# A new planned order, stores of two adjacent pieces in one transfer, and stores split over unequal row counts, in a cross-covariance attention with a mixture of adapters

## The chip, the cores and the metric

The kernel runs on one core of a Trainium2 chip. The metric is the device time of one execution in microseconds, lower is better. The core has five engines with their own instruction streams: TensorE (PE in the profile) for matrix products, VectorE (DVE), ScalarE (ACT), GpSimd (POOL) and SyncE (SP). The last two compute next to nothing here: GpSimd issues the loads and SyncE the stores. Sixteen transfer engines move the data between device memory and the on-chip memory.

## What is computed

Four batches of q, k and v, each of 6400 rows and 256 columns, are reduced to one 256 x 256 attention matrix per batch. Its product with v goes through a mixture of eight low-rank adapters, two of which are chosen for every row.

```python
qn = q / (np.linalg.norm(q, axis=1, keepdims=True) + 1e-06)     # norm over the 6400 rows
kn = k / (np.linalg.norm(k, axis=1, keepdims=True) + 1e-06)
s = kn.transpose(0, 2, 1) @ qn / tau                            # 256 x 256 per batch
a = softmax(s)                                                  # over the last axis
x = (v @ a).reshape(25600, 256)
logits = x @ w_gate                                             # 8 experts
topk, w = the two largest logits of a row, and their softmax
delta = sum over the two of w * (x @ A[e]) @ B[e]               # rank 16
out = x + delta
```

q, k and v are float32, 26.2 MB each, and so is the output of 26.2 MB. All of q and k of a batch must be there before its matrix a is known; only then can v of that batch be turned into output.

## The kernel before

**Tiling.** The 6400 rows of a batch are laid out as 128 partitions by 50 columns ("chunks"), each of 256 values; a column of all partitions is 128 KB in float32. q and k come in three loads each of 17, 17 and 16 columns (`QK`), some of them cut further (`PARTS`). v comes in five pieces of 10 columns (`NP`, `PC`). GpSimd's transfers convert to bf16 on the way (`do_load`). Output is written from y buffers of 10 columns in float32 (`do_store`), and goes out from SyncE, one store for each piece. The last two pieces of the last batch are stored in parts of 4, 4 and 2 columns (`FINE`, `UNITS`).

**Steps.** For q and k: `do_G` adds each chunk to the 256 x 256 product in two accumulators, and to the sums of squares, which are the diagonals of k'k and q'q. For the groups of chunks named in `OFF` these sums of squares are not made by TensorE but by ScalarE (`do_sq`), VectorE (`do_add`, `do_red`) and two small products (`do_n2p`). Then follow a short chain per batch (`n2`, `rsqrt`, `rq_ps`, `s`, `exp`, `aT_ps`, `waA_ps`, `waA`, `a`), which ends in the matrix a in bf16 and in its products with the gate's and the adapters' weights. For v: `T` transposes a piece, `ZL` (or `log` and `Z`) gives gate logits and adapter values, a few VectorE steps choose two experts, `Ze` weights the adapter values, `gzT` transposes them, `Y` makes the output of two chunks from four products of v with a and two with the adapters' B, and `Ye` copies it from PSUM into the y buffer. Pieces in `MERGED` make logits and adapter values in one product `ZL`; the others make `log` first and `Z` later. `Te`, `ZLe`, `gzTe` and `Ye` are copies that may go to ScalarE or VectorE, as the planner decides (`copy`).

**Order.** The order of every instruction is written out by a planner in the kernel file (class `Plan`), which runs when the program is built. It holds a cost for each step, a fixed number of buffers of each kind (`STORE`: 6 for q and k, 3 for v, 7 for y, and so on), and one rank for each step that follows from the order of the loads (`WORDS`) and from how far transposes run ahead (`AHEAD`). It then plays the kernel through; the order in which steps start in it is the order of the instructions, and the buffer that a step took in it is the buffer of the program. Transfers are modelled as two streams that share a rate. `WARM` matmuls on constant data are put in where TensorE would be idle, so that its clock stays up.

**Stores behind loads.** `HOLD` names stores that shall wait until a certain load has landed, so that this load and those ahead of it have the transfer engines for themselves. The kernel before does this with a transfer of its own: `do_hold` copies 16 values of the loaded tile into a scrap tile from SyncE, which must wait for the load, and stores stand behind it in SyncE's order:

```python
def do_hold(s, kind, b, i):
    ...
    nc.sync.dma_start(scrap, src)

def do_store(s, b, i, c, n):
    lo = i * PC + c
    nc.sync.dma_start(out_v[b, :, lo:lo + n, :], held["y", (b, i), ""][:, c:c + n, :])
```

**Queues.** Loads are issued in the order of `WORDS`; each waits on GpSimd until its buffer is free. Stores are issued in order on SyncE; each waits until its piece is complete. At most eight transfers of one issuing path are under way at once: a ninth waits until the one eight places ahead of it has landed.

Of the kernel before, what the change touches and what calls it, by code (L numbers as in the profile page):

```python
# [18 lines left out]
class Step:  # L19
# [3 lines left out]
    def __init__(self, key, eng, deps, rank, take, give, size=0.0):  # L23
        self.packet = max(size, 0.08)
        self.key, self.eng, self.deps, self.rank = key, eng, deps, rank
        self.take, self.give, self.size = take, give, size
        self.users, self.place = [], {}
        self.ready, self.end, self.on = 0.0, None, None
        self.left = len(deps)
        self.only = next(iter(eng)) if len(eng) == 1 else None  # L30


class Clock:


    WINDOW, FIRST, LOW, HIGH = 3.413, 0.31, 0.5, 0.8
# [32 lines left out]
class Plan:  # L69

    LAT = 0.07
    DMA_LAT = 1.8
    ENGINES = ("PE", "DVE", "ACT", "POOL", "SP")
    ISSUE = 0.55
    ISSUE_LAT = 1.8
    STORE_LAT = 1.4
    OUT = 8

# [15 lines left out]

    def run(self, head):
# [4 lines left out]
        loads, queue, stores = list(self.loads), [], []  # L100
        now, out, left = 0.0, 0, sum(s.key[0] != "warm" for s in self.steps.values())
        free["POOL"] = 0.2
        clock = Clock()

# [5 lines left out]
        def can_take(s):  # L110
            return all((kind, name) in held or self.store[kind] for kind, name in s.take)

        def start(s, eng):
            for kind, name in s.take:
                if (kind, name) not in held:
                    held[kind, name] = self.store[kind].pop(0)
                    s.place[kind] = held[kind, name]
            s.on = eng
            s.t = now
            self.out.append(s)  # L120

# [5 lines left out]
        while left:  # L127
            again = False
            if (loads and free["POOL"] <= now + 1e-9 and out < self.OUT and can_take(loads[0])):
                s = loads.pop(0)  # L130
                start(s, "POOL")
                out += 1
                free["POOL"] = now + self.ISSUE
                push(free["POOL"], "free", None)
                push(now + self.ISSUE_LAT, "asked", s)
                again = True
            for e in self.ENGINES:
# [3 lines left out]
                for s in wait[e]:  # L141
                    if not can_take(s) or (s.key[0] == "warm" and not clock.idle(now)):
                        continue
# [3 lines left out]
                    if best is None or (s.rank, s.seq) < (best.rank, best.seq):  # L147
                        best = s
# [9 lines left out]
                else:  # L158
                    push(free[e], "end", best)
# [3 lines left out]
            busy = [x for x in (queue, stores) if x]  # L163
            t = events[0][0] if events else float("inf")
            base = max(now, head)

            share = sum(x[0].packet for x in busy)
            if busy:
                t = min(t, base + min(x[0].size / x[0].packet for x in busy) * share)
            assert t < float("inf"), [s.key for s in self.steps.values() if s.end is None][:20]  # L170
            if t > base:
                for x in busy:
                    x[0].size -= (t - base) * x[0].packet / share
                    if x[0].size < 1e-6:
                        push(t + self.DMA_LAT, "landed", x[0])
                        out -= x is queue
                        x.pop(0)
            now = max(now, t)
            while events and events[0][0] <= now + 1e-9:
                _, _, what, s = heapq.heappop(events)  # L180
                if what == "asked":
                    queue.append(s)
                elif what == "store":
                    stores.append(s)
# [3 lines left out]
                elif what == "landed":  # L188
                    push(now + (SAFE if s.on == "POOL" else 0.0), "end", s)
                    for u in s.users:  # L190
                        if u.key[0] == "hold":
                            u.left -= 1
                            if u.left == 0:
                                push(now, "ready", u)
                elif what == "end":
# [6 lines left out]
                    for u in s.users:  # L202
                        u.left -= u.key[0] != "hold"
                        if u.left == 0 and u.eng and u.key[0] != "hold":
                            push(now + (0.0 if s.on == u.only else self.LAT), "ready", u)
# [10 lines left out]
V = ((0, 1), (1, 1), (2, 1), (3, 1), (4, 1))  # L216
# [13 lines left out]

def make_plan(B, order, ahead):
# [6 lines left out]
    for kind, b, i in order:  # L238
        if kind == "v":
            p.add(("load", "v", b, i, V[i][0] * PC, V[i][1] * PC), {}, (), 0, take=(("v", (b, i)),),  # L240
                  size=LOAD * V[i][1] * PC + 0.062)
            continue
        for c, n in PARTS.get((b, i), QK[i:i + 1]):
            for h in "qk":
                p.add(("load", h, b, i, c, n), {}, (), 0, take=(("qk", (h, b, i)),), size=LOAD * n + 0.062)

    for h in "qk":
        p.add(("cast", h), {"ACT": 0.6}, [("load", h, 0, 0) + PARTS[0, 0][0]], 0)
    p.loads[2].size += 0.5
    for b in range(B):  # L250

        for i, (c0, n) in enumerate(QK):
            for c in range(c0, c0 + n):
# [8 lines left out]
                p.add(("G", b, c), {"PE": 0.442 - 0.112 * sum((b, group_of(c), w) in OFF for w in "kq")}, deps,  # L262
# [4 lines left out]
        for w in "kq":  # L267
# [5 lines left out]
            for x, g in enumerate(halves):  # L273
                c, n = GROUPS[g]
                i = max(i for i, q in enumerate(QK) if q[0] <= c)
                p.add(("sq", w, b, g), {"ACT": 0.2 + 0.2125 * n},
                      [k for k in p.steps if k[:4] == ("load", w, b, i) and k[4] < c + n and c < k[4] + k[5]]
                      + [("cast", w)] * ((b, c) == (0, 0)), pos["qk", b, i] - SQ, take=(("ssq", (w, b)) if x == 0 else ("sq", (w, b, g)),),
                      give=(("qk", (w, b, i)),))
                if x:  # L280
                    p.add(("add", w, b, g), {"DVE": 0.15 + 0.268 * n},
# [4 lines left out]
            if halves:  # L286
                p.add(("red", w, b), {"DVE": 1.9}, [before], pos["qk", b, len(QK) - 1] - 1, give=(("ssq", (w, b)),))
# [699 lines left out]
```

## Time and profile before

| | |
|---|---|
| time, median of three runs | 254.41 us (254.39 to 254.47) |
| span of the profiled run | 252.7 us |
| TensorE busy (matmul) | 217.8 us, 86% |
| VectorE busy | 192.7 us, 76% |
| ScalarE busy | 151.1 us, 60% |
| loads: share of the 16 transfer engines | 74.4%, 6,912 packets |
| stores and small transfers: share | 26.1%, 3,968 packets |
| device memory read and written | 78.91 MB and 26.21 MB, 416 GB/s over the span |

The span is the time from the first to the last instruction of the profiled execution. The share of a queue is the time that its packets took, as a share of sixteen engines over the span; packets of one engine may overlap a little, so the sum can pass 100%. A packet of a load or a store is one row: what one partition receives or gives in one transfer. The bytes of a load are counted as written, in bf16, while twice as many are read. A line such as "POOL v L578 <- PE T_ps L788" means that an instruction of GpSimd which writes v, from line 578, stood idle until an instruction of TensorE that writes T_ps was done.

### The profile page before, as it was taken

To read this page: it belongs to the slowest core of one execution; us is meant where nothing else is said; L and a number is where in the kernel's file an instruction comes from. 1 tells how busy PE (TensorE), PEld (TensorE's weight loads), DVE (VectorE), ACT (ScalarE), POOL (GpSimd) and SP (SyncE) were. 2 spreads that over 40 slices of the span, in tenths; PEclk is the share of its full clock that TensorE was granted. 3 is DMA by queue.
4 is the path that set the end of the run, shared out by engine and by line. 5 is a ranking of instruction groups with operands and counts; after the bars stand their busy time and mean duration, and the time that the engine had idled before them with its cause. 6 is when DMAs were issued, how large, how long until landed. Compare 5 with 4: busy or idle time off the path is not lost.

```text
span 252.7 us, 5852 instructions
## 1 busy us (share of the span) xinstructions
PE 217.8 (86%) x2357; PEld 193.0 (76%) x2357; DVE 192.7 (76%) x528; ACT 151.1 (60%) x269; POOL 27.1 (11%) x54
## 2 busy tenths in 40 slices
PE   0274995988999998689999999889999979999990
PEld 0162882876999996579899899779999769999980
DVE  0055589869899987588899899489898898889850
ACT  5454427546786543975667768362674846657671
POOL 7003010040002002000500100500000000000000
PEclk9998899999999999999999999999999999999997
DMA  8999999999999999999999999999999999999996
GB/s 251 217 217 209 211 223 208 217 218 215 215 217 241 303 305 298 224 213 221 210 215 220 215 217 217 211 212 313 317 251 353 322 341 317 337 392 415 404 408 249
DMA packets 11243, 66.70 MB, mean 264 GB/s; under 512 B 1360, under 2 KB 1744, under 8 KB 6608
## 3 DMA queue, kind: packets, MB, share of 16 engines
q0 software_dynamic: 6912, 38.80, 74.4%
q1 hardware_dynamic: 3968, 26.87, 26.1%
q10 hardware_dynamic: 336, 0.66, 0.8%
q8 instruction: 18, 0.29, 0.4%
q14 instruction: 9, 0.07, 0.1%
HBM read 78.91 MB, written 26.21 MB: 416 GB/s over the span
## 4 chain that ended last, share of the span: by engine, by line
PE 53%; DMA 32%; issue 5%; DVE 4%; ACT 2%; POOL 1%; POOLq 0%; DVEq 0%
DMA v<-in_v_dram 18%; PE Y_ps L915 13%; PE acc L593 10%; DMA qk<-in_q_dram 10%; PE Y_ps L920 6%; PE T_ps L788 5%; PE ZL_ps L812 5%; DMA qk<-in_k_dram 5%; PE gzT_ps L902 4%; PE acc L597 3%; PE acc L602 2%; PE Z_ps L879 1%; ACT a_exp L715 1%; DVE a_bf L763 1%; PE log_ps L826 1%
## 5 line engine op out<-in xcount | busy, mean ns | idle before, releaser
L593 PE MATMUL acc<-qk 128*128 128x256 bf16 x400 | 69.6, 282 | 17.0 <-DMA qk<-in_k_dram 9.4
L915 PE MATMUL Y_ps<-a_bf,vT 128*128 128x256 bf16 x400 | 60.0, 273 | 0.2 <-DVE acc_sb L710 0.2
L621 DVE TENSOR_TENSOR ssq<-ssq,sq 128x1280 f32<-128x1280 f32 (+1 forms) x27 | 43.4, 1606 | 19.6 <-ACT sq L615 19.6
L769 ACT COPY y<-Y_ps 128x512 f32<-128x512 f32 x79 | 46.2, 586 | 16.6 <-PE Y_ps L920 13.5
L593 PEld LDWEIGHTS <-qk 128*128 128x128 bf16 x400 | 34.2, 101 | 20.7 <-DMA qk<-in_k_dram 11.5
L615 ACT ACTIVATE sq<-qk 128x1280 f32<-128x1280 bf16 (+1 forms) x27 | 36.9, 1368 | 17.7 <-DVE ssq L621 16.6
L915 PEld LDWEIGHTS <-vT 128*128 128x128 bf16 x400 | 38.9, 98 | 4.7 <-issue 0.3
L920 PE MATMUL Y_ps<-ball,gzT 128*128 128x256 bf16 x200 | 38.2, 273 | 0.0
L597 PE MATMUL acc<-qk 128*128 128x128 bf16 x242 | 34.5, 224 | 0.0
L788 PE MATMUL T_ps<-ident,v 128*128 128x128 f32 x200 | 27.6, 274 | 0.6 <-DVE waA_sb L757 0.4
L769 ACT COPY vT<-T_ps 128x512 f32<-128x512 f32 (+1 forms) x44 | 21.2, 510 | 10.9 <-PE T_ps L788 10.5
L597 PEld LDWEIGHTS <-qk 128*128 128x128 bf16 x242 | 24.4, 101 | 3.5
L890 DVE TENSOR_TENSOR gz<-zl,gateg 128x256 bf16<-128x256 f32 x70 | 26.3, 445 | 0.3
L578 POOL DMA_DIRECT2D v<-in_v_dram x20 | 11.5, 576 | 133.7 <-PE T_ps L788 92.8
L788 PEld LDWEIGHTS T_ps<-ident,v 128*128 128x128 f32 x200 | 22.3, 141 | 1.6 <-DVE waA_sb L757 0.6
L602 PE MATMUL acc<-qk 128*128 128x128 bf16 x168 | 23.4, 222 | 0.0
L902 PE MATMUL gzT_ps<-ident,gz 128*128 128x128 f32 x100 | 20.9, 281 | 2.6 <-DVE gateg L868 1.4
L920 PEld LDWEIGHTS <-gzT 128*128 128x128 bf16 x200 | 19.6, 98 | 2.3
L812 PE MATMUL ZL_ps<-waA_sb,vT 128*128 128x136 bf16 x280 | 19.5, 223 | 1.7 <-DVE waA_sb L757 1.5
L771 DVE COPY gzT<-gzT_ps 128x256 f32<-128x256 f32 (+1 forms) x40 | 15.0, 380 | 7.1 <-PE gzT_ps L902 5.6
L812 PEld LDWEIGHTS <-vT 128*128 128x128 bf16 x280 | 17.7, 98 | 2.4 <-issue 2.1
L615 ACT ACTIVATE ssq<-qk 128x1536 f32<-128x1536 bf16 x8 | 11.9, 1489 | 11.4 <-DMA qk<-in_q_dram 7.4
(80 smaller groups left out, 271.3 us busy)
## 6 DMA issues: line engine op xcount, KB each, us to landing
out_dram<-y SPq DMA_DIRECT2D x18, 1280.0 KB, 16.7
v<-in_v_dram POOLq DMA_DIRECT2D x20, 640.0 KB, 20.5
qk<-in_q_dram POOLq DMA_DIRECT2D x7, 1088.0 KB, 23.7
qk<-in_k_dram POOLq DMA_DIRECT2D x7, 1088.0 KB, 28.4
qk<-in_q_dram POOLq DMA_DIRECT2D x4, 512.0 KB, 19.2
qk<-in_k_dram POOLq DMA_DIRECT2D x4, 512.0 KB, 22.5
qk<-in_q_dram POOLq DMA_DIRECT2D x2, 1024.0 KB, 19.4
qk<-in_k_dram POOLq DMA_DIRECT2D x2, 1024.0 KB, 23.8
```

The source lines that it names most:

```text
L593: nc.tensor.matmul(acc[ic][:, 0:256], kt[:, j, ic::CC], qt[:, j, :], start=c == 0, stop=False, skip_group_check=True)
L597: nc.tensor.matmul(acc[ic][:, 256:384], kt[:, j, ic::CC], kt[:, j, ic::CC], start=False, stop=False, skip_group_check=True)
L602: nc.tensor.matmul(acc[ic][:, 384:512], qt[:, j, ic * P:(ic + 1) * P], qt[:, j, ic * P:(ic + 1) * P], start=False, stop=c == NC - 1, skip_ ...
L615: nc.scalar.activation(out[:, 0:n, :], t[:, j:j + n, :], ACT.Square)
L621: nc.vector.tensor_tensor(out=t, in0=t, in1=held["sq", (w, b, g), ""][:, 0:n, :], op=OP.add)
L769: nc.scalar.copy(out, in_)
L788: nc.tensor.matmul(ps[:, j, :], vt[:, c + j, :].bitcast(FP32), W["ident32"], is_transpose=True, start=(j == 0), stop=(j == n - 1))
L812: nc.tensor.matmul(ps[:, j, :], vT_of(b, i, c + j)[:, :, ic], st[b]["waA"][:, ic, :], start=(j == 0 and ic == 0), stop=(j == n - 1 and ic ...
L890: nc.vector.tensor_tensor(out=pairs[:, h].rearrange("p c (e r) -> p c e r", e=E), in0=z[:, 2 * h:2 * h + 2, :].rearrange("p c (e r) -> p c ...
L902: nc.tensor.matmul(ps[:, j, :], pairs[:, j * P:(j + 1) * P], W["ident32"], is_transpose=True, start=(j == 0), stop=(j == n // 2 - 1))
L915: nc.tensor.matmul(ps[:, j, :], vT_of(b, i, c + j)[:, :, ic], st[b]["a"][:, ic, :], start=(j == 0 and ic == 0), stop=False, skip_group_che ...
L920: nc.tensor.matmul(ps[:, j, :], pair[:, :, j], W["B"], start=False, stop=(j == 1), skip_group_check=True)
```

## The change

The transfers and the planner that orders everything are changed; the arithmetic is the same.

- Five pairs of adjacent pieces (`PAIRS`) take two adjacent y buffers and leave in one store of 20 columns. For that, all y buffers become one tile and all v buffers another, and the planner looks for adjacent free places (`find`).
- Three entries in `SPLIT` name stores that leave in four transfers of 112, 6, 6 and 4 rows (`SHARES`), to give transfer engines unequal shares.
- `HOLD` is new in content, and a held store now depends on the load itself, without a transfer of its own.
- The planner's model of transfers follows single rows of two rings in turn, with a cost for each row and for each completion, and a spread of completions that grows with time. Its costs of steps are revised.
- The order of loads (`WORDS`), the sets `OFF` and `MERGED`, and the constants `AHEAD`, `SQ`, `SAFE` and `HEAD` are new.

The diff, cut to its core:

```diff
+PAIRS = {(0, 3), (1, 1), (1, 3), (2, 0), (3, 1)}
...
+def pieces(b, i):
+    return next((((b, j), (b, j + 1)) for j in (i - 1, i) if (b, j) in PAIRS), ((b, i),))
...
-            parts = UNITS if b == B - 1 and i >= NP - FINE else ((0, PC),)
+            names = pieces(b, i)
+            if (b, i) != names[0]:
+                continue
+            parts = UNITS if b == B - 1 and i >= NP - FINE else ((0, PC * len(names)),)
...
-WORDS = ('q10 v00 v01 v02 q11 v03 q12 v04 v10 v11 q20 v12 v13 v14 q21 v20 v21 v22 q22 q30 '
-         'q31 q32 v23 v24 v30 v31 v32 v33 v34')
+WORDS = ('q10 v00 v01 q11 v02 v03 q12 v04 q20 v10 q21 v11 q22 v12 v13 v14 v20 q30 q31 v21 v22 q32 v23 v24 v30 '
+         'v31 v32 v33 v34')
-AHEAD = 2.7
+AHEAD = 1.9
-HOLD = {(0, 0): ('k', 3, 1), (0, 1): ('k', 1, 2), (0, 4): ('k', 3, 2), (1, 0): ('k', 3, 1),
-        (1, 1): ('k', 3, 2), (1, 2): ('k', 3, 2), (1, 3): ('k', 3, 2), (1, 4): ('k', 3, 2),
-        (2, 0): ('k', 3, 1), (2, 1): ('k', 3, 2), (2, 4): ('k', 3, 1)}
+HOLD = {(0, 0): ('v', 3, 4), (0, 1): ('k', 3, 0), (0, 2): ('k', 3, 0), (0, 3): ('v', 3, 2), (0, 4): ('v', 1,
+        4), (1, 0): ('v', 1, 3), (1, 1): ('v', 1, 3), (1, 2): ('k', 1, 0), (1, 3): ('v', 2, 3), (1, 4):
+        ('v', 3, 1), (2, 0): ('v', 2, 4), (2, 2): ('v', 1, 3), (3, 2): ('v', 3, 2), (3, 3): ('v', 3, 4), (3,
+        4): ('v', 2, 3)}
+SPLIT, SHARES = {(0, 0), (1, 4), (3, 0)}, (112, 6, 6, 4)
...
-SQ = 2
-SAFE = 0.5
+SQ = 4.0
+SAFE = 2
...
+    Y = sbuf.tile([P, STORE["y"] * PC, C], FP32, name="y")
+    VS = sbuf.tile([P, STORE["v"] * PC, C], BF16, name="v")
...
-        nc.sync.dma_start(out_v[b, :, lo:lo + n, :], held["y", (b, i), ""][:, c:c + n, :])
+        at_y = at["y", (b, i)] * PC + c
+        p = 0
+        for rows in SHARES if (b, i) in SPLIT else (P,):
+            r = nc.sync.dma_start(out_v[b, p:p + rows, lo:lo + n, :], Y[p:p + rows, at_y:at_y + n, :])
+            if (b, i) in HOLD and not p:
+                tc.add_manual_dep(r.ins, loaded[held_by(plan, b, i)],
...
+            p += rows
```

`OFF` goes from 35 entries (195 chunk sums) to 33 (185), `MERGED` from 14 pieces to 13. The first loads are the same in both: four columns of q and of k from SyncE and ScalarE, the other thirteen from GpSimd.

In the order that the planner makes, the stores of the kernel before begin with the pieces (0,2), (0,1), (0,3), (0,0), (1,0) and (2,0), batch first, and go on in order from (0,4). Those of the changed kernel are: (1,0); (1,1) with (1,2); (0,1); (0,2); (1,3) with (1,4); (2,0) with (2,1); (2,2); (2,3); (0,3) with (0,4); (2,4); (3,0); (0,0); (3,1) with (3,2); and then (3,3) and (3,4) in parts of 4, 4 and 2 columns.

## The prediction

> **What bounds the kernel now.** I read the page's slices and queues first, then the windows at the head, in the middle and at the tail, then the chain and the waits. The page shows what the transfer engines do over the whole span:
>
> ```profile
> PE   0274995988999998689999999889999979999990
> DMA  8999999999999999999999999999999999999996
> GB/s 251 217 217 209 211 223 208 217 218 215 215 217 241 303 305 298 224 213 221 210 215 220 215 217 217 211 212 313 317 251 353 322 341 317 337 392 415 404 408 249
> q0 software_dynamic: 6912, 38.80, 74.4%
> q1 hardware_dynamic: 3968, 26.87, 26.1%
> HBM read 78.91 MB, written 26.21 MB: 416 GB/s over the span
> ```
>
> The DMA row is full from the second slice to the last but one, and the loads' share and the stores' share add up to 100.5% of 16 engines' span. A pure load stretch shows some 215 GB/s because a load is counted at its two-byte size; it reads twice that. TensorE is also near full from about 100 us on, but a single engine at 86% beside a queue at 100% says that transfers come first. The windows show where the transfer engines are not full (columns: stretch, length, busy time of the engines, clock, DMA share, GB/s):
>
> ```profile
> 0.00:1.00 1.00, 0.00 (x0) 0.00 (x0) 0.00 (x0) 0.00 (x0) 0.20 (x4) 1.00 0.05 4
> 1.00:2.00 1.00, 0.00 (x0) 0.00 (x0) 0.00 (x0) 0.19 (x1) 0.58 (x1) 1.00 0.80 127
> ...
> 110.00:160.00 50.00, 49.61 (x533) 45.52 (x531) 42.87 (x106) 34.50 (x62) 4.77 (x9) 1.00 1.04 216
> ...
> 238.00:239.00 1.00, 1.00 (x18) 0.99 (x16) 0.71 (x2) 0.77 (x3) 0.00 (x0) 1.00 0.83 338
> 239.00:240.00 1.00, 1.00 (x13) 0.90 (x11) 1.00 (x4) 0.17 (x1) 0.00 (x0) 1.00 0.85 356
> ...
> 249.00:250.00 1.00, 0.00 (x0) 0.00 (x0) 0.00 (x0) 0.00 (x0) 0.00 (x0) 0.59 0.85 338
> 250.00:251.00 1.00, 0.00 (x0) 0.00 (x0) 0.00 (x0) 0.00 (x0) 0.00 (x0) 0.50 0.34 133
> 251.00:252.00 1.00, 0.00 (x0) 0.00 (x0) 0.00 (x0) 0.00 (x0) 0.00 (x0) 0.50 0.06 25
> ```
>
> Three gaps are to be seen. The head costs 0.95 + 0.20 = 1.15 us. Near 239 us there is a hole of about 0.17 + 0.15, with the 0.90 share of the next window some 0.4 us in all. At the tail the 16 engines don't end together: from 249.0 on the mean engine works 0.85 + 0.34 + 0.06 = 1.25 us, so it ends at 250.25, and the slowest at about 251.5. The semaphore records agree: the last store's 16 completions come between 249.95 and 251.95 us, ten of them 0.37 to 2.00 us after the first, six within 0.15 us. So in a kernel that is bound by transfers the end is set by the mean work of an engine, by holes, and by how far the slowest engine lags.
>
> The chain and one wait:
>
> ```profile
> 246.55 0.23 PE Y_ps L920 x2
> 246.78 0.02 issue
> 246.81 0.59 ACT y L769
> ```
>
> ```profile
> POOL v L578 <- PE T_ps L788: 92.8, 11, 17.7
> ```
>
> TensorE ends at 246.78, the last copy into y at 247.40 and the span at 252.7: both resources end together, transfers a little later. GpSimd's long waits for T cost nothing as long as the DMA row stays full, which it does.
>
> **What the Trainium skill says.** "DMA: Bandwidth & Descriptors", section "Issuing engines are not separate DMA queues", says that transfers of all issuers run on the same 16 engines and interleave. The trace agrees: the two queues' shares add up to one full set. The same page, section "Specifications", puts HBM at about 358 GB/s for one core and the fabric at 435; the trace has 416 over the span and 2 x 216 = 432 in loads, so the second is the nearer ceiling and I take measured rates. Section "Why a DMA increments its semaphore by 16 and not by 1" says that a transfer issued by SyncE uses the largest count of engines up to 16 that divides its rows, the lowest-numbered ones. No transfer of the kernel before shows that split at this size: 112 rows would be 7 on each engine, 6 rows one each on engines 0 to 5, 4 rows one each on 0 to 3. Section "Queues, rings and completion order" says that an engine takes turns between its rings by packet; a 20-column row would then hold up a load row for longer.
>
> **The change, part by part.**
>
> Pairs. Five pairs become one store each, so each engine moves 40 rows fewer, of twice the size. What a row costs beyond its bytes is taken from the trace's packet records: over 5 us windows a store row of 10,240 bytes takes 390 ns of an engine's time, while load rows read 26.9 bytes per ns, which would be 381 ns; store rows of 4,096 and 2,048 bytes (about 167 and 84 ns) are 15 and 8 ns over the same line. So 9 to 12 ns a row, and 40 rows give 0.36 to 0.48 us. I take 0.45. No 20,480-byte row is in the trace; the lower bound is 0.
>
> Split stores. SPLIT names (0,0), (1,4) and (3,0), but (1,4) is the second piece of the pair (1,3), and its store carries the name (1,3): in the program built from the change only two stores of 112 rows stand on SyncE. Each takes a row (0.39 us) from engines 6 to 15 and gives two to engines 0 to 3 and one to 4 and 5. Over two stores: -0.78, +1.56 and +0.78 us. If the six early engines of the trace are 0 to 5, the late ten end at up to 2.00 - 0.78 = 1.22 us and the early four at about 1.56, so the last completion comes 2.0 - 1.6 = 0.4 us earlier. If a late engine is among 0 to 3, it ends at up to 3.5, which is 1.5 later. That engine numbers can't be seen in this trace is the largest unknown; six being early, as the shares suppose, speaks for the first. I take -0.4.
>
> Order. Loads carry the same bytes; the seven v loads behind the last q and k are the same. The hole at 239 us is a store that was not ready; with stores kept back for the end (the store of (0,0) waits for the last v load) I expect most of it filled: -0.3 us, bounds 0 and -0.4.
>
> Holds. Three transfers of 32 bytes and the SyncE waits for them go; the waits now sit on the stores themselves. Stores queue in order on SyncE, so what stands behind a held store waits too, and through y slots so does the copy of Y. Six small extra transfers of 0.33 us issue each are hidden behind stores of 3 us. Together 0.
>
> TensorE and the others. OFF drops from 195 to 185 chunk sums, each worth two 128-column matmuls (0.11 us): +1.1 us. MERGED drops from 14 to 13; a merged piece has twenty ZL matmuls in 1.18 us, another one log 0.50 and Z 1.12: +0.4. Warm-up matmuls fall from 39 to 19. TensorE is idle or warming up for some 43 us of the span, so 1.5 us can be hidden; behind the last waA_ps the work falls from 40.1 to 38.8 us, because five instead of three of the last seven pieces are merged. Twenty gzT copies move from VectorE (76% busy) to ScalarE (60%). I put these at 0 for the end.
>
> The sum: -0.45 - 0.4 - 0.3 = -1.15. I give 0.1 back for the pair of (3,1) and (3,2), which can't start until both pieces are done. The span is 1.7 us shorter than the time in both (252.7 against 254.41), so the forecast is 254.4 - 1.05, about 253.4 us.
>
> **Rivals.**
>
> TensorE becomes the end. After Y of (3,2) it has 9.9 us of work (ten Y groups of 0.655, T, ZL and gzT), while transfers still to come are 40 columns, 12.5 us at 3.12 per ten. With 0.6 us to the copy's end and 1.2 from issue to first packets (the head's 1.15), the mean engine can't end before TensorE's end + 0.6 + 1.2 + 12.5 - 9.9, that is 4.4 us behind it; today it ends 3.5 behind. A gain of 0.75 in the mean asks TensorE to end at about 245.1 instead of 246.8. For it: the shorter tail, and loads of batch 3 that come earlier in the new order. Against: more work in all, and full windows from 110 us on. If it ends where it does now, the mean engine ends 0.9 later and the skew gives 0.4 back; halfway between is about 254.3, no change.
>
> A hole in the middle. Stores now begin behind the load of (1,3), near 122 us by the load order at 3.06 us per ten columns, where they began at 76.6. Until then y's seven slots fill; once they are full, Y stops, vT and v slots stay taken, loads stop, and held stores may not fill the gap. Against it: the kernel before kept the queue full through 92.8 us of such waits. One hole of 2 to 3 us, or a split that falls on the late engines, gives about 255.7, slower.
>
> All of it is had: 0.48 + 0.4 + 0.4, and a skew that falls by 0.3 more, gives 252.8.
>
> **How the numbers follow.** The forecast of about 253.4 has 0.5, the full gain 0.13, TensorE at the end 0.17, a hole or a wrong split 0.2. Under 253.9 lie the first two and a little of the third: faster 0.66. The rest of the third within half a microsecond of now, with a little of the fourth: same 0.14. Slower 0.2. The range leaves out half of the slow case and the very best: 252.6 to 255.4.
>
> **What would show it.** Right: store packets of 20,480 bytes near 765 to 775 ns; a DMA row without a hole at 239 us; the last store's completions within 1.6 us; TensorE ending near 245.3. Wrong: a DMA share under 0.9 between 80 and 240 us; GpSimd waiting for T or SyncE for a held load while that share is low; completions spread by 3 us; TensorE ending at or after 246.8.

## The result, and the profile after

The changed kernel takes 258.16 us (median of 4 runs, 257.86 to 258.56) where the kernel before takes 254.4: a ratio of 1.0148, with a 95% interval of 1.0131 to 1.0166. It is 3.8 us slower. The forecast was 253.4, and the time lies outside the range of 252.6 to 255.4 too.

The page of the changed kernel, with the rows that answer to those shown of before:

```profile
PE   0774995899999899889999995899899899999960
...
DMA  8999999999999999999999999999999999999696
GB/s 248 210 217 207 214 220 213 222 217 208 218 214 216 213 217 217 217 213 212 214 309 215 216 329 322 317 288 214 215 298 391 342 315 316 422 302 352 271 389 242
...
q0 software_dynamic: 6912, 38.80, 73.6%
q1 hardware_dynamic: 3184, 26.87, 25.9%
...
HBM read 78.91 MB, written 26.21 MB: 409 GB/s over the span
```

The span is 256.8 us. The load packets (second column of a queue) are as many as before, the store packets 784 fewer, and the bytes the same. The work of the transfer engines did fall. This is an estimate from the packet records: if every packet is charged the time that its kind takes undisturbed, an engine's mean work is about 248.4 us before and 247.9 after. But the DMA row now has a 6 in the third slice from the end, and TensorE's clock is at half near 160 us. The windows show both (columns: stretch, length, busy time of PE, PEld, DVE, ACT and POOL, clock, DMA share, GB/s):

```profile
160.00:168.00 8.00, 6.55 (x53) 5.92 (x54) 2.96 (x3) 4.22 (x7) 0.00 (x0) 0.57 1.03 316
232.00:234.00 2.00, 2.00 (x30) 1.94 (x28) 1.27 (x5) 1.93 (x6) 0.00 (x0) 1.00 1.02 404
234.00:236.00 2.00, 2.00 (x21) 1.78 (x20) 1.76 (x9) 1.54 (x4) 0.00 (x0) 1.00 1.06 336
236.00:238.00 2.00, 2.00 (x21) 1.91 (x19) 1.97 (x6) 1.51 (x4) 0.00 (x0) 1.00 0.71 256
238.00:240.00 2.00, 2.00 (x30) 1.97 (x28) 1.52 (x5) 1.91 (x6) 0.00 (x0) 1.00 0.34 132
240.00:242.00 2.00, 2.00 (x21) 1.79 (x20) 1.76 (x10) 1.54 (x5) 0.00 (x0) 1.00 0.61 236
254.00:256.00 2.00, 0.00 (x0) 0.00 (x0) 0.00 (x0) 0.00 (x0) 0.00 (x0) 0.50 0.15 59
```

From 232 us on only stores are under way. At full rate they move about 430 GB/s: 433 in the window from 234 to 236 us of e1_unsplit below, and sixteen rows of 10,240 bytes in 385 ns are 426. So 336, 256, 132 and 236 mean that (94 + 174 + 298 + 194) / 430 x 2 us = 3.5 us are lost between 234 and 242. TensorE is busy in all of it: the data are being made. For the most part a transfer is missing, and SyncE's own instructions say why. This is the line of the stores, from 232.5 us to the issue of the pair (3,1) and (3,2) (count, then shortest, median and longest duration in ns):

```profile
L973 SPq DMA_DIRECT2D out_dram<-y x5: 322/1552/2811, 232.5 to 239.2; - x5
```

One by one, from the records of SyncE (start and duration in us):

```
store          rows   start   took        store          rows   start   took
(3,0)          112   225.24   0.34        (0,0)          112   232.55   0.32
(3,0)            6   225.64   1.66        (0,0)            6   232.91   2.81
(3,0)            6   227.35   1.38        (0,0)            6   235.77   1.81
(3,0)            4   228.77   1.39        (0,0)            4   237.63   1.43
                                          (3,1)+(3,2)    128   239.17   1.55
```

The parts of six and four rows keep SyncE for 1.4 to 2.8 us each. The pair is complete at 237.8 us, but SyncE is free for it only at 239.1, its issue takes 1.55, and its first rows start at 241.2. Then forty columns of stores follow, 12.5 us at 3.12 per ten, and the first completion of the last store comes at 254.24. TensorE ends at 248.06 and the last store is issued at 248.7, so the end is set by what is queued, not by TensorE.

A missing transfer is not all of it. In the window from 234 to 236 us the DMA share is 1.06 and yet only 336 GB/s are moved: the engines are busy there, with rows that take too long. The packet records tell the two parts of the loss apart. Behind the last row of a load, where only stores are under way, a row of 10,240 bytes takes 385 ns in the median, before and after. Before, 4 of 798 such rows took over 450 ns; in the changed kernel it is 27 of 243, the longest 1.96 us. What they took beyond 385 ns is 0.96 us for the mean of sixteen engines (0.06 before), and from 231.9 to 242 us the mean engine has no packet under way for 2.65 us (0.36 before). Together this is the loss of 3.5 us.

This is the end of the chain of waits, and GpSimd's wait for T, against 246.78 and 92.8 us before:

```profile
247.84 0.23 PE Y_ps L962 x2
248.09 0.59 ACT y L812
```

```profile
POOL v L629 <- PE T_ps L830: 111.0, 13, 26.1
```

GpSimd's waits for T are 18 us longer. Between 130 and 212 us they cost as little as before: with packets charged as above, no stretch of 2 us there is used by less than 0.98. The stretch ahead of it, from 124 to 128 us, comes up again below.

### The profile page after: what moved, and what is told of

Same layout as the page of the kernel before. It is cut to its first block, busy times and chain, and to the rows that moved or that the text cites. A ratio compares the mean times of both kernels' runs of the same rounds, so it can differ in the third digit from the quotient of the medians.

```text
span 256.8 us, 5860 instructions
## 1 busy us (share of the span) xinstructions
PE 221.6 (86%) x2377; PEld 196.3 (76%) x2377; DVE 177.4 (69%) x501; ACT 157.0 (61%) x289; POOL 27.2 (11%) x54
## 4 chain that ended last, share of the span: by engine, by line
DMA 43%; PE 29%; issue 13%; DVE 8%; ACT 2%; POOL 2%; POOLq 0%; ACTq 0%
DMA qk<-in_k_dram 28%; DMA v<-in_v_dram 15%; PE Y_ps L957 8%; PE Y_ps L962 4%; PE ZL_ps L854 4%; PE acc L644 3%; PE T_ps L830 3%; PE gzT_ps L944 3%; DVE ssq L672 3%; POOL qk L629 1%; PE acc L653 1%; DVE ssq L678 1%; DVE gz L932 1%; PE Z_ps L921 1%; PE acc L648 1%
## 5 line engine op out<-in xcount | busy, mean ns | idle before, releaser
L644 PE MATMUL acc<-qk 128*128 128x256 bf16 x400 | 75.5, 286 | 17.4 <-DMA qk<-in_k_dram 10.9
L672 DVE TENSOR_TENSOR ssq<-ssq,sq 128x1280 f32<-128x1280 f32 (+1 forms) x25 | 40.4, 1615 | 29.3 <-ACT sq L666 27.7
L644 PEld LDWEIGHTS <-qk 128*128 128x128 bf16 x400 | 35.7, 104 | 21.2 <-DMA qk<-in_k_dram 12.6
L666 ACT ACTIVATE sq<-qk 128x1280 f32<-128x1280 bf16 (+1 forms) x25 | 34.4, 1374 | 23.5 <-DVE ssq L672 10.9
L957 PEld LDWEIGHTS <-vT 128*128 128x128 bf16 x400 | 39.3, 99 | 4.2
L653 PE MATMUL acc<-qk 128*128 128x128 bf16 x252 | 36.2, 227 | 0.0
L812 ACT COPY vT<-T_ps 128x512 f32<-128x512 f32 (+1 forms) x47 | 23.9, 533 | 14.1 <-PE T_ps L830 13.6
L830 PE MATMUL T_ps<-ident,v 128*128 128x128 f32 x200 | 29.5, 274 | 0.8 <-DMA v<-in_v_dram 0.8
L648 PE MATMUL acc<-qk 128*128 128x128 bf16 x178 | 27.1, 237 | 0.0
L653 PEld LDWEIGHTS <-qk 128*128 128x128 bf16 x252 | 23.8, 102 | 1.9
L932 DVE TENSOR_TENSOR gz<-zl,gateg 128x256 bf16<-128x256 f32 x65 | 23.5, 445 | 0.4
L812 ACT COPY gzT<-gzT_ps 128x256 f32<-128x256 f32 (+1 forms) x40 | 13.4, 346 | 14.4 <-PE gzT_ps L944 14.1
L648 PEld LDWEIGHTS <-qk 128*128 128x128 bf16 x178 | 19.3, 108 | 3.8
```

The source lines that it names most:

```text
L644: nc.tensor.matmul(acc[ic][:, 0:256], kt[:, j, ic::CC], qt[:, j, :], start=c == 0, stop=False, skip_group_check=True)
L648: nc.tensor.matmul(acc[ic][:, 256:384], kt[:, j, ic::CC], kt[:, j, ic::CC], start=False, stop=False, skip_group_check=True)
L653: nc.tensor.matmul(acc[ic][:, 384:512], qt[:, j, ic * P:(ic + 1) * P], qt[:, j, ic * P:(ic + 1) * P], start=False, stop=c == NC - 1, skip_ ...
L666: nc.scalar.activation(out[:, 0:n, :], t[:, j:j + n, :], ACT.Square)
L672: nc.vector.tensor_tensor(out=t, in0=t, in1=held["sq", (w, b, g), ""][:, 0:n, :], op=OP.add)
L812: nc.scalar.copy(out, in_)
```

## The experiments

The theories of the loss are these. A: the small parts of split stores hold SyncE, and what stands behind them comes late; the rivals within it are that they are slow because they use fewer than sixteen engines, or because one transfer follows close on another. B: TensorE comes late and sets the end. C: the rows of 20,480 bytes hold up loads that TensorE waits for. D: TensorE's half clock near 160 us (the first window above, clock 0.57) makes everything late. E: these loads are late because stores share the engines with them at all. F and G: the hold on store (1,0) and the pair at the end leave holes of their own. Ratios below are to the kernel before, with 95% intervals. Where the intervals of two runs overlap, their difference is not clear of noise. This holds of e2_unpair, e3_warm and e13_smallfirst against the changed kernel, and of e6_split16, e7_tail and e9_split22 against e1_unsplit.

**Whole stores (e1_unsplit).** Program order of all engines stays.

```diff
-SPLIT, SHARES = {(0, 0), (1, 4), (3, 0)}, (112, 6, 6, 4)
+SPLIT, SHARES = set(), (112, 6, 6, 4)
```

> The changed kernel, order kept, with the two stores of 112, 6, 6 and 4 rows sent whole again. Theory A: the small transfers of 6 and 4 rows occupy SyncE for 1.4 to 2.8 us each, six in a row before the pair of (3,1) and (3,2), and hold that pair back to 239.2 us although its last copy ended at 237.8. Then all issues take about 0.35 us, the pair is issued near 237.9, its packets begin near 239, the hole from 236 to 242 us shrinks by 1.5 to 2.5 us, and the time falls from 258.2 to about 256.0. Theory B: the end is set by TensorE, which comes about 3 us late out of a load of k that lands at 161.4 us; the small transfers only fill time. Then TensorE still ends at 248.1 and the time stays at 257.6 or more.

Measured: 255.39 us (254.65 to 257.5, 17 runs), ratio 1.0046 (1.0029 to 1.0064). So the six extra transfers cost 2.8 us of the 3.8. TensorE ends at 247.46, only 0.6 us earlier, so B falls. The stores' line, and five windows:

```profile
L973 SPq DMA_DIRECT2D out_dram<-y x19: 332/333/913, 124.2 to 248.1; - x19
```

```profile
124.00:126.00 2.00, 2.00 (x29) 1.92 (x27) 2.00 (x3) 1.24 (x4) 0.83 (x2) 1.00 1.04 185
126.00:128.00 2.00, 2.00 (x32) 1.95 (x30) 1.93 (x8) 1.76 (x2) 1.02 (x2) 1.00 1.10 179
...
234.00:236.00 2.00, 2.00 (x21) 1.80 (x19) 1.82 (x8) 1.48 (x4) 0.00 (x0) 1.00 1.05 433
236.00:238.00 2.00, 2.00 (x21) 1.96 (x20) 1.97 (x7) 1.93 (x4) 0.00 (x0) 1.00 0.70 296
238.00:240.00 2.00, 2.00 (x30) 1.91 (x28) 1.45 (x6) 1.60 (x5) 0.00 (x0) 1.00 1.16 492
```

The median issue is 0.333 us now, the pair goes out at 237.2, and the slow rows are gone (1 of 265 over 450 ns): from 234 to 236 us the share is as in the changed kernel, and the rate 433 GB/s instead of 336. Two holes stay: near 237 us, and at 124 to 128, where loads alone move 185 and 179 GB/s instead of 216. The DMA share is above 1 in the latter all the same: packets that share an engine overlap in the record, so a hole in a stretch of loads shows in the GB/s column.

**Split stores in the kernel before (e5_before_split).** Its stores (2,4) and (3,0) leave in 112, 6, 6 and 4 rows.

```diff
-        nc.sync.dma_start(out_v[b, :, lo:lo + n, :], held["y", (b, i), ""][:, c:c + n, :])
+        p = 0
+        for rows in (112, 6, 6, 4) if (b, i) in ((2, 4), (3, 0)) else (P,):
+            nc.sync.dma_start(out_v[b, p:p + rows, lo:lo + n, :], held["y", (b, i), ""][p:p + rows, c:c + n, :])
+            p += rows
```

> The kernel before, with the stores of (2,4) and (3,0) alone sent in 112, 6, 6 and 4 rows. There the next store on SyncE comes some 6 us later each time, so that up to 5 us of issue should be hidden. Theory A: each transfer of 6 or 4 rows takes 1.2 to 2.8 us of SyncE here too, against 0.33 for the others. On shares there are two readings: if the early engines are the low-numbered ones, as the change supposes, the 16 completions of the last store close up from 2.0 to about 1.6 us and the time is 254.0 to 254.2; if not, they spread to 2.5 us or more and the time is 254.9 or more; the same time as before would mean that the shares don't reach the end.

Measured: 256.46 us (256.39 to 257.0), ratio 1.0081 (1.0068 to 1.0094): 2.1 us slower than without the split. But the issues are short, and a wait stands in their place:

```profile
L930 SPq DMA_DIRECT2D out_dram<-y x9: 252/322/426, 219.3 to 236.4; - x9
```

```profile
SPq L930 <- DMA out_dram<-y: 8.6, 3, 3.2
```

```profile
234.00:236.00 2.00, 2.00 (x27) 1.88 (x26) 1.86 (x6) 1.28 (x3) 0.00 (x0) 1.00 0.93 323
236.00:238.00 2.00, 2.00 (x21) 1.82 (x19) 1.48 (x7) 1.80 (x4) 0.00 (x0) 1.00 0.90 317
```

A small part takes one of the eight places like a large one. At 230.4, 233.5 and 236.4 us SyncE waited for the transfer eight places ahead to land (8.6 us in all), so the store of (3,1), issued at 233.2 us in the kernel before, went at 236.4. Yet these waits cost next to nothing in the sum: from 231.9 to 242 us the mean engine has nothing under way for 0.40 us, where it was 0.36, since the hole that the kernel before had near 239 is gone. Two other things cost. 54 of 794 rows behind the last load are slow, 1.02 us for the mean engine against 0.06; that is why the windows show 323 and 317 GB/s at shares of 0.93 and 0.90. And the last store's completions are spread over 3.4 us, the last of them 2.2 us behind their mean, where it was 1.3. The two come to 1.9 us. Whether the shares fall on engines that lag already isn't shown, since the records don't number the engines. So splitting lost here in two ways, neither of them slow issue.

**Parts of 112 and 16 rows (e6_split16).** Sixteen rows use all sixteen engines; the part leaves sixteen completion records.

```diff
-(112, 6, 6, 4)
+(112, 16)
```

> The changed kernel, order kept, with the two split stores in 112 and 16 rows instead of 112, 6, 6 and 4: both parts can use all 16 engines, a row on each. Theory A1: it is the transfer with fewer than 16 engines that is slow to issue; then every issue takes 0.33 to 0.5 us, the pair of (3,1) and (3,2) is issued near 238, and the time is that of the unsplit order, 255.2 to 255.8. Theory A2: any further transfer behind a full queue is slow to issue; then the 16-row parts take 1.2 us or more each, and the time is 256 to 257.

Measured: 256.34 us (255.55 to 256.67), ratio 1.0062 (1.0045 to 1.0079), between whole stores and four parts. The two parts of 16 rows took 0.62 and 2.16 us to issue. So it isn't the number of engines below sixteen that makes a part slow. Nor is SyncE what costs here: it is free at 233.9, and the pair goes out at 236.1, earlier than in e1_unsplit. The engines are busy and move too little, where they move some 430 GB/s with whole rows:

```profile
234.00:236.00 2.00, 2.00 (x21) 1.88 (x19) 1.89 (x6) 1.48 (x5) 0.00 (x0) 1.00 1.01 358
236.00:238.00 2.00, 2.00 (x30) 1.99 (x29) 1.52 (x6) 1.91 (x6) 0.00 (x0) 1.00 0.98 363
```

Rows are slow again, 30 of 261 behind the last load, and the last store's completions are spread over 3.5 us instead of 1.8.

**Small parts first (e13_smallfirst).**

```diff
-(112, 6, 6, 4)
+(4, 6, 6, 112)
```

> The changed kernel with the parts of its two split stores the other way round, 4, 6, 6 and then 112 rows. If a small part is slow to issue because a large part was issued just before it, the first small ones now take 0.25 to 0.45 us, SyncE is free for the pair (3,1) and (3,2) at about 237.8 and the time is 255.4 to 256.5. If any transfer of less than 16 engines that comes close behind another is slow there, three of the four of each store still take 1.4 to 2.8 us: 257.5 to 258.6, as in the changed kernel.

Measured: 257.72 us (257.13 to 260.01), ratio 1.0142 (1.0106 to 1.0179), as slow as the changed kernel. The issues of (3,0) took 0.33, 0.61, 0.63 and 0.57 us, those of (0,0) 0.25, 1.55, 1.26 and 0.62. The first of a store is quick and those close behind it are not, the large part among them. The pair is out at 236.7, earlier than in e1_unsplit, and yet there is a hole, earlier too:

```profile
234.00:236.00 2.00, 2.00 (x21) 1.81 (x19) 1.86 (x8) 1.47 (x4) 0.00 (x0) 1.00 0.45 147
```

Now it is the part of 112 rows that comes late, at 235.1 instead of 232.6. Whatever stands behind the small parts pays. And 61 of 247 rows are slow, the most of any run.

**One split elsewhere (e9_split22).** `SPLIT` names (2,2) alone.

```diff
-SPLIT, SHARES = {(0, 0), (1, 4), (3, 0)}, (112, 6, 6, 4)
+SPLIT, SHARES = {(2, 2)}, (112, 6, 6, 4)
```

> The changed kernel, order kept, with one split store only: that of (2,2) at 206.8 us, behind which SyncE issues nothing for 7 us, in 112, 6, 6 and 4 rows. Theory A: a split costs time by what waits on SyncE behind its small transfers; here nothing does for up to 6 us, so the time is that of the unsplit order, 254.9 to 255.8, or lower by up to 0.4 us if its shares help. Rival: rows that run on six or four engines cost the end as such, since these engines get 3 rows more than the rest; then the time is 256 or more although SyncE is free.

Measured: 256.02 us (255.31 to 256.19), ratio 1.0064 (1.0050 to 1.0079). Here all four parts were quick:

```profile
L973 SPq DMA_DIRECT2D out_dram<-y x4: 275/358/400, 205.9 to 207.0; - x4
```

And yet the median is 0.6 above whole stores, on the side that speaks against splits; the intervals overlap, so this may be nothing. No gain is to be seen.

**The split stores side by side.** Slow rows are those of 10,240 bytes that start behind the last load and take over 450 ns. Their excess over 385 ns, and the idle time from 231.9 to 242 us (sixteen less the packets under way at each moment), are us of the mean of sixteen engines, all from the packet records of one execution.

```
run                split near the end   slow rows    longest   excess   idle
before             no                    4 of 798     0.77      0.06    0.36
e1_unsplit         no                    1 of 265     0.79      0.03    0.49
e9_split22         no, at 206            2 of 269     0.78      0.04    0.12
changed kernel     yes                  27 of 243     1.96      0.96    2.65
e13_smallfirst     yes                  61 of 247     1.32      1.30    1.37
e6_split16         yes                  30 of 261     1.11      0.64    0.20
e5_before_split    yes                  54 of 794     1.32      1.02    0.40
```

So theory A is a part of the story. In the changed kernel the late pair makes most of the idle time. The slow rows come with every split store in a stretch of stores alone, whatever SyncE does, and with no other store: in the other runs with whole stores at the end at most two rows are slow. Beside loads few show: from 206 to 218 us of e9_split22, where (2,2) is split, 4 of 211 rows are slow. Of each run this is one execution.

**Pairs as two stores each (e2_unpair).** Splits stay.

```diff
-            r = nc.sync.dma_start(out_v[b, p:p + rows, lo:lo + n, :], Y[p:p + rows, at_y:at_y + n, :])
+            m = min(n, PC)
+            r = nc.sync.dma_start(out_v[b, p:p + rows, lo:lo + m, :], Y[p:p + rows, at_y:at_y + m, :])
+            if n > PC:
+                nc.sync.dma_start(out_v[b, p:p + rows, lo + PC:lo + n, :], Y[p:p + rows, at_y + PC:at_y + n, :])
```

> The changed kernel, order kept, with each store of 20 columns sent as two of 10 columns right after each other; the split stores stay. Theory C: rows of 20,480 bytes hold a transfer engine for 0.77 us between two load rows of 0.65 us, where rows of 10,240 bytes hold it for 0.39, and so delay the load of k for chunks 17 to 33 of the last batch, on which TensorE waits at 161.4 us. Then this load lands near 157.5 to 158.5 us, TensorE doesn't fall under half use before it, the half clock from 160 to 167 us goes, TensorE ends 2 to 3 us earlier (245 to 246), and the time falls to 255.5 to 256.5. Rival: the pair's size plays no part, the loads are late since stores are let go behind v of (1,3) at all; then the load lands at 160.5 or later, TensorE's end moves by less than 0.5 us and the time rises by 0.3 to 0.5 us for 40 more rows on each engine.

Measured: 259.18 us (258.15 to 259.67), ratio 1.0174 (1.0146 to 1.0201). The mean work of an engine, estimated as above, rises by 0.4 us and the time by 1.0. The load of k that TensorE waits for near 160 us lands later (163.4 against 161.4), not earlier, so shorter rows don't help it. They are not tested alone, though: the first half of the pair (1,1) now goes out at 139.0, where the pair went at 144.7, and takes engine time from the loads sooner. For C nothing speaks.

**TensorE kept warm (e3_warm).** Eleven matmuls on constant data ahead of ZL of (2,0), where TensorE stood idle for 2.7 us in the changed kernel; a few lines put them into the list of steps.

```diff
+EXTRA = [(("ZL", 2, 0, 0), 11)]
```

> The changed kernel with eleven matmuls on constant data put into TensorE's order ahead of the first ZL of piece (2,0), where it waits for the load of k at 158.7 to 161.4 us. Theory D: the idle time itself is small, but it drops TensorE to half clock from 160.4 to 167.2 us, which costs 3.4 us of its work once; then the clock stays at 1.0 there, TensorE ends 2.0 to 3.0 us earlier (245 to 246), and the time falls by 1 to 2.5 us. Rival: TensorE has slack behind that point or the tail is held by SyncE; then the clock stays up and the time moves by less than 0.5 us.

Measured: 257.67 us (257.51 to 258.33), ratio 1.0128 (1.0106 to 1.0151). The clock is whole from 45 to 250 us, TensorE ends 0.7 us earlier and the time falls by 0.5. So seven microseconds at half clock cost 0.5 or less. I read it as slack, which is argued and not shown: from 180 to 199 us of the changed kernel VectorE is busy for 9.5 to 9.7 us of ten, in large part with the sums of squares, and TensorE must follow it. D is a small part.

```profile
180.00:190.00 10.00, 9.00 (x106) 7.84 (x104) 9.54 (x23) 7.21 (x12) 0.53 (x1) 1.00 1.09 238
190.00:200.00 10.00, 9.27 (x119) 8.53 (x117) 9.72 (x32) 6.26 (x13) 0.99 (x2) 1.00 0.99 372
```

**Stores held for that load (e4_holdk31).** The pair (1,1) and all behind it wait until the second load of k of batch 3 has landed.

```diff
-loaded[held_by(plan, b, i)]
+loaded[held_by(plan, b, i) if (b, i) != (1, 1) else ("load", "k", 3, 1, 17, 17)]
```

> The changed kernel, order kept, with the store of the pair (1,1) and (1,2), and so everything behind it on SyncE, held until the load of k for chunks 17 to 33 of the last batch has landed, in place of the load of v for (1,3). Theory E: this load is late because three stores share the engines with it, whatever their row size. Then it lands near 154 us, TensorE isn't idle at 159 us, the half clock from 160 to 167 us goes and TensorE ends 2 to 3 us earlier; time about 256. Rival: y buffers run out while the stores are held, the copies of Y of (1,3) start later than 161 us and TensorE stands just as long; then the end of TensorE moves by less than 1 us and the time stays within 1 us of 258.2.

Measured: 262.14 us (259.95 to 263.1), ratio 1.0283 (1.0232 to 1.0334). The load lands 5.7 us earlier, at 155.7, and the kernel is 4 us slower:

```profile
164.00:174.00 10.00, 3.69 (x22) 2.96 (x22) 2.91 (x10) 2.68 (x7) 0.00 (x0) 0.50 1.02 337
```

The pair lands at 169.65 instead of 160.65. Until then its y buffers are taken, Y can't be copied out, and TensorE works 3.7 us of ten at half clock. It ends at 253.2. So E is right about the load and no help for the time.

**The hold on (1,0) off (e8_free10)**, with whole stores; the planned order stays.

```diff
-            if (b, i) in HOLD and not p:
+            if (b, i) in HOLD and (b, i) != (1, 0) and not p:
```

> The unsplit order with the store of (1,0) let go as soon as it is complete, not held behind the load of v for (1,3). In the unsplit order the transfer engines moved about 0.9 us less than they could between 124 and 130 us: loads wait for v buffers there and the only store that is complete is held until 124. Theory F: with (1,0) on its way earlier this hole is filled and the time falls by 0.4 to 0.9 us. Rival: (1,0) takes the engines from the loads of v ahead of it by just as much, so that the hole only moves: the time stays within 0.3 us.

Measured: 254.33 us (254.02 to 255.98, 13 runs), ratio 1.0000 (0.9987 to 1.0012), 1.06 less than with the hold.

```profile
124.00:126.00 2.00, 2.00 (x28) 1.92 (x26) 2.00 (x4) 1.14 (x3) 0.32 (x1) 1.00 1.02 321
126.00:128.00 2.00, 2.00 (x32) 1.94 (x31) 1.93 (x7) 1.39 (x2) 1.06 (x2) 1.00 1.04 348
```

The store is issued at 120.8 instead of 124.2, and its rows fill what was a hole. TensorE's wait for k falls from 2.8 to 1.1 us, its clock stays whole at 161 us, and it ends at 245.13, 2.3 us earlier.

**The pair (3,1) and (3,2) as two stores (e7_tail)**, with whole stores.

```diff
-            r = nc.sync.dma_start(out_v[b, p:p + rows, lo:lo + n, :], Y[p:p + rows, at_y:at_y + n, :])
+            m = PC if (b, i) == (3, 1) else n
+            r = nc.sync.dma_start(out_v[b, p:p + rows, lo:lo + m, :], Y[p:p + rows, at_y:at_y + m, :])
+            if n > m:
+                nc.sync.dma_start(out_v[b, p:p + rows, lo + m:lo + n, :], Y[p:p + rows, at_y + m:at_y + n, :])
```

> The unsplit order with the pair of (3,1) and (3,2) alone sent as two stores of 10 columns; the other four pairs stay. In the unsplit order the engines still stood partly idle from 236 to 238 us, about 0.5 us in the mean, since (3,1), done at about 231, waited for (3,2), done at 237. Theory G: with (3,1) sent on its own this hole closes and the time falls by 0.3 to 0.6 us, to about 254.9. Rival: TensorE's end at 247.5 carries the last parts anyway; then the hole moves behind it and the time stays at 255.2 to 255.6.

Measured: 255.03 us (254.87 to 255.82, 8 runs), ratio 1.0025 (1.0013 to 1.0037), 0.36 less than as a pair. The hole near 237 us is gone:

```profile
236.00:238.00 2.00, 2.00 (x22) 1.97 (x20) 1.97 (x7) 1.93 (x5) 0.00 (x0) 1.00 1.01 424
```

**Put together (e10_best; e11_best22; e12_bestwarm).** e10_best makes the edits of e1_unsplit, e7_tail and e8_free10; e11_best22 splits (2,2) as well; e12_bestwarm is e10_best with the eleven matmuls of e3_warm.

```diff
-SPLIT, SHARES = {(0, 0), (1, 4), (3, 0)}, (112, 6, 6, 4)
+SPLIT, SHARES = set(), (112, 6, 6, 4)
...
+            m = PC if (b, i) == (3, 1) else n
...
+            if (b, i) in HOLD and (b, i) != (1, 0) and not p:
```

> The unsplit order with both edits that helped: (1,0) not held, and the pair of (3,1) and (3,2) sent as two stores. If the two gains are of different places, they add: 254.3 less 0.3 to 0.4, about 254.0, faster than the kernel before by 0.2% or so. If the hole in the tail is already closed by the earlier end of TensorE, the time stays at 254.2 to 254.4.

> The same as the run with both edits, with the store of (2,2) alone in 112, 6, 6 and 4 rows. In the run with (1,0) let go the last completions were spread over 3.1 us, six engines early by 0.9 or more. If the early ones are the low-numbered, the spread falls to about 2.7 and the time by 0.2 to 0.4 us, to about 253.7; if not, the spread grows to 3.4 or more and the time rises by 0.3 or more.

> The changed order with whole stores, the pair (3,1) and (3,2) stored as two, the hold of (1,0) off, and eleven constant-data matmuls ahead of ZL of (2,0). If the half clock at 161 us is what took back the gains of the two edits when they were put together (255.0 us, TensorE ending at 246.8, where the hold alone gave 254.33 and TensorE ended at 245.1): the clock stays whole, TensorE ends near 246, and the time is 254.0 to 254.5. If TensorE's end isn't what sets the time there, because a chain on VectorE follows between 180 and 199 us and because transfers have no more holes: 254.8 to 255.2, as without the matmuls.

Measured: 255.0 us (254.47 to 255.98, 21 runs), ratio 1.0017 (1.0009 to 1.0026); 254.56 (254.03 to 256.39, 22 runs), ratio 1.0011 (1.0000 to 1.0022); 255.17 (254.63 to 255.77, 10 runs), ratio 1.0029 (1.0015 to 1.0042). The gains didn't add. The split of (2,2) in e11_best22 changes nothing clear. In e10_best the half clock at 161 us is back and TensorE ends at 246.80. In e12_bestwarm the clock stays whole, TensorE still ends at 247.61, and the time is no better; so the clock alone isn't what took the gain back. The intervals of e8_free10 and e10_best overlap, and why e8_free10 is the fastest of these orders stays open. None beats the kernel before; e8_free10 equals it.

## Why the prediction was wrong

**The step that failed** is "Six small extra transfers of 0.33 us issue each are hidden behind stores of 3 us. Together 0." It took the issue of a whole store as the price of a small one, and it put the price on the transfer engines, where a row is small, and not on SyncE, where a transfer of six rows took up to 2.81 us, against 0.33 for one of 128 in the median, and stands ahead of the next. Measured in place, the six issues took 10.5 us of SyncE (1.66 + 1.38 + 1.39 + 2.81 + 1.81 + 1.43). The first three were hidden, behind stores already queued. During the last three the queue ran dry, since the pair behind them was not issued: 2.65 us of idle time (0.49 with whole stores), most of the loss of 3.5. The transfer engines were not free of cost either: rows of the stretch took up to 1.96 us instead of 0.385, another 0.96 us, a term that the prediction doesn't have. By e1_unsplit the splits cost 2.8 us of time in all.

The rest is the hold on (1,0), 1.06 us by e8_free10, which ends at 254.33. This was measured with whole stores; the profile of the changed kernel itself has a shallower hole there (203 and 223 GB/s at 124 to 128 us). The time of e8_free10 is no better than before although the pairs are in it, so the new order gives back elsewhere about what the pairs bring; where, the runs don't show.

**Split stores, -0.4.** Nothing of it was had. The changed kernel's last completion is 1.3 us behind the mean of its sixteen, as before, and in e5_before_split it is 2.2. The stated doubt, that engine numbers can't be seen, was the right doubt. That a small transfer runs on few engines is seen: the parts of six rows leave seven completion records and those of four rows five. The Trainium skill says so in "DMA: Bandwidth & Descriptors", section "Why a DMA increments its semaphore by 16 and not by 1": only the engines that a transfer uses post a completion, and the issuer writes the rest at once. The trace agrees: the first record of each part comes 0.13 to 0.17 us after its issue ends, long before the rows land.

**Pairs, -0.45.** Right in the work: rows of 20,480 bytes take 774 ns in the median (765 to 775 were expected) against twice 398 for the half rows, and with stores alone (e1_unsplit, after 234 us) 764 against twice 385. That is 6 to 22 ns a row, where 9 to 12 were expected, and the mean work fell by an estimated 0.5 us. In the time, undoing the pairs lost 1.0 and the give-back for the last pair, 0.1, measured 0.36, but neither is clear of noise.

**Order, -0.3 for the hole at 239 us.** Wrong in sign with splits, and open with whole stores, where a hole of 0.3 to 0.5 us (296 GB/s at 236 to 238, 492 behind it; 0.49 us of idle time) stays until the last pair is taken apart.

**Holds, 0.** Wrong by 1.06: the hold on (1,0) alone leaves loads that can't fill the engines at 124 to 128 us. The rival "a hole in the middle", near 122 us, named this place and the split as well, and gave 255.7 for one of them; both came and made 258.2. The hole cost less than the 2 to 3 us named, and the split came in another way than by late engines. The rival had been given a chance of 0.2.

**TensorE, 0.** It ends 1.3 us later than before, where 245.3 was hoped for, but six microseconds of stores are queued behind it, and 0.5 us or less is what the half clock cost there. The shorter tail came as forecast: from the last waA_ps to its end TensorE takes 40.8 us instead of 43.4. But that product is done at 207.3 us instead of 203.4, though the last row of q and k lands at 182.6 before and 182.5 after, and this was not foreseen. In e8_free10 it is 204.4, and TensorE ends at 245.1. VectorE's sums of squares between 180 and 199 us are the likely reason; no run tests it.

**Not settled.** Why an issue takes 0.25 to 0.4 us in one place and 0.6 to 2.8 in another. Fewer than sixteen engines is not it, the size of the transfer ahead is not it alone, and the transfer eight places ahead had landed. Small size is not it either: in the changed kernel a whole pair issued at 214.3 us, close behind another store, took 1.73. Nor does the count of rows still queued tell them apart: 52 to 241 rows were outstanding at the slow parts of the changed kernel, 128 to 133 at the quick ones of e9_split22 and 491 to 497 at those of (2,4) in e5_before_split. And open is why rows of split stores are slow where only stores are under way.

## What to carry to other kernels

A transfer has two prices on its issuing queue, the time of its issue and its place among those that may be under way, and both are charged to what stands behind it; a part of four rows can pay as much as a store of 128, or more. Before a store is split, look for the next store in that queue and when it is ready. Then look at the rows themselves: in a stretch of stores alone, a DMA share near 1 with too few GB/s beside it (1.06 with 336 here) went with rows that took too long, not with a missing transfer. A hold on a store is a bet that the loads ahead can fill the engines alone, and the GB/s of that stretch against the best load rate tells whether they do.

## What the hardware showed that was not expected

Issues of stores took from 0.25 to 2.81 us on one queue, with nothing waited for in the record. Rows of 10,240 bytes took up to 1.96 us instead of 0.385 where stores of fewer than 128 rows ran with no load beside them. A fetch of instructions of 16 KB is one packet of 0.88 to 0.98 us in the changed kernel; whether such fetches make single engines lag isn't shown. And these orders scatter more from run to run than the kernel before did: 254.65 to 257.5 us for whole stores, 254.13 to 255.29 for before.
